# The first token group: four x transfers, applies on VectorE alone, w1's sums of squares added by TensorE

## The chip, the cores and the metric

The kernel runs on one core of a Trainium2 chip. A core has TensorE (PE: matmuls and transposes, results in PSUM), VectorE (DVE), ScalarE (ACT), GpSimd (POOL) and SyncE (SP, which here only issues transfers). Each engine works through its own instructions in order and waits for others by semaphores. The metric is the device time of one execution in microseconds, the median of several runs.

## The reference

The input x has 2048 tokens of 448 channels. Three things are added up:

```python
xn = layernorm(x)
y  = irfft2(rfft2(xn) * (w_r + 1j * w_i))        # spectral part
h  = gelu(layernorm(x) @ w1)                     # 448 x 448
hs = concat(shift(h[:, 0:112], +1), shift(h[:, 112:224], -1),
            shift(h[:, 224:336], +2), shift(h[:, 336:448], -2)) @ w2
x1 = x + hs
b  = x1 + gelu(layernorm(x1) @ w3) @ w4          # 448 x 1792 and back
out = x + y + b
```

The shifts are along the tokens. Everything is float32 outside; inside, each operand of a matmul is split into a high and a low float16 half, and three products (high x high, high x low, low x high) stand for one.

## The kernel before

Tokens are held as 16 blocks of 128 (token = 16 a + b, with a on the partitions and b the block), in four groups of four blocks, `GRP`. Group 0 is blocks 14, 15, 0, 1. Weights are scaled by a power of two before they are split: the scale comes from the sum of squares of the whole matrix (`squares` on ACT gives one sum per partition, `powers` adds them up over columns and partitions and makes the scale and its inverse from the exponent).

The part that is touched is the preamble, until the first matmul with w1, and goes like this:

- SP issues the loads in order (lines 195 to 223): x of group 0 in two transfers of two blocks each (line 200), w1 in four slices of up to 128 rows (lines 206 and 207), x of group 1, a second copy of w1's last slice, w2, x of group 2, w3, x of group 3. There are eight completion counters that are used in turn; a transfer waits until the one eight before it has landed.
- PE runs `WARM` = 22 matmuls on a zeroed tile, whose results nobody reads (line 890).
- `norm1(0, ...)`: DVE takes mean and variance of each block (lines 316 and 317), then four-element-wide operations: variance + eps in two forms (lines 342 and 343), a first guess of the inverse root by integer arithmetic in two instructions (344 and 345), minus mean times the guess (347). Then the blocks are normalised in place, x * y + m (the "applies"): block 14 on POOL, 15 and 0 on DVE (line 360), block 1 shared between POOL (128 columns, line 355) and ACT (320 columns, line 357). The refinement of the guess (`refine`) is done on POOL much later, and is folded into a scale after the matmul.
- Meanwhile ACT squares w1's four slices (`squares1`, line 246), each an activation with a read-out of its accumulator. Then `powers` (lines 248 to 266): a reduction over the columns on DVE (251), a matmul with a matrix of ones (258), which adds over partitions, and three operations on DVE: the exponent (261), the scale s1 (263), the inverse r1 (264).
- `warm_on` (line 943): one small matmul that reads the result of line 347, and two more warm-up matmuls behind it.
- `turn_pe(0, t)` transposes 128 columns of all four blocks on PE; `turn_copy` takes the high half out of PSUM on ACT (line 424) and the low half on DVE (425). `split_w` scales and splits w1's slices (lines 273 and 275 on DVE for the first slice, ACT and POOL for the others). The matmuls with w1 are at line 465.

Instructions are placed on the engines by the framework's planner, by program order and a timeline that it estimates; `with behind(...)` adds an order between two instructions of one engine without a wait between engines. In the preamble most of the order is fixed that way: the ones matmul stands behind the four transposes of `turn_pe(0, 0)` on PE, `turn_pe(0, 1)` behind the ones matmul, and the first w1 matmuls follow.

Of the kernel before, what the change touches and what calls it, by code (L numbers as in the profile page):

```python
# [12 lines left out]
F32 = mybir.dt.float32  # L13
F16 = mybir.dt.float16
I32 = mybir.dt.int32
AF = mybir.ActivationFunctionType
# [10 lines left out]
WARM = 22  # L27
# [95 lines left out]
def body(tc, nc, x, wf, w1, w2, w3, w4, c_g, c_n, c_small, out):  # L123
# [41 lines left out]
    def xb(b):  # L165
        g, i = WHERE[b]
        return xt[g][:, i]
# [27 lines left out]
    def load_x(g):  # L195
        if g:
            SY.dma_start(xt[g], xv[:, GRP[g][0]:GRP[g][0] + 4])
        else:
            for i in (0, 2):
                SY.dma_start(xt[g][:, i:i + 2], xv[:, GRP[g][i]:GRP[g][i] + 2])  # L200
# [47 lines left out]
    def powers(m, n, key, tag="acc", mid=None, pin=None, down=0):  # L248

        t = pc.tile([128, 1], F32, name=f"pt{key}")  # L250
        i = V.tensor_reduce(out=t, in_=m[:, :n + 1], axis=AX.X, op=ALU.add)
        after["t" + key] = (i.ins,)
        if mid:
            with behind("t" + key):
                mid()
        pm = bank(tag, f"pm{key}") if isinstance(tag, str) else tag
        with behind(*pin) if pin else contextlib.nullcontext():
            i = T.matmul(pm[:, 0:1], ones, t, start=True, stop=True)
        after["p" + key] = (i.ins,)
        e = pc.tile([128, 3], I32, name=f"pe{key}")  # L260
        V.tensor_scalar(out=e[:, 0:1], in0=pm.bitcast(I32)[:, 0:1], scalar1=1, scalar2=0x7F800000,
                        op0=ALU.logical_shift_right, op1=ALU.bitwise_and)
        V.tensor_scalar(out=e[:, 1:2], in0=e[:, 0:1], scalar1=-1, scalar2=(185 - down) << 23, op0=ALU.mult, op1=ALU.add)
        i = V.tensor_scalar(out=e[:, 2:3], in0=e[:, 0:1], scalar1=1, scalar2=(69 + down) << 23, op0=ALU.mult, op1=ALU.add)
        after["s" + key] = (i.ins,)
        return e.bitcast(F32)[:, 1:2], e.bitcast(F32)[:, 2:3]
# [28 lines left out]

    def rsqrt(r, a, n, key):
# [3 lines left out]
        V.tensor_single_scalar(i, a.bitcast(I32), 1, op=ALU.logical_shift_right)  # L300
        V.tensor_scalar(out=i, in0=i, scalar1=-1, scalar2=0x5F3759DF, op0=ALU.mult, op1=ALU.add)
# [29 lines left out]
    def norm1(g, apply, seen=0, mid=None):  # L331
# [8 lines left out]
        y = yi.bitcast(F32)  # L340
        with behind(0, 3) if g == 2 else contextlib.nullcontext():
            V.tensor_scalar(out=a[:, n:], in0=mv[:, :n, 1], scalar1=1.0 + EPS, scalar2=EPS * EPS, op0=ALU.mult, op1=ALU.add)
            V.tensor_scalar(out=a[:, 0:n], in0=mv[:, :n, 1], scalar1=EPS, scalar2=None, op0=ALU.add)
        V.tensor_single_scalar(yi, a.bitcast(I32), 1, op=ALU.logical_shift_right)
        V.tensor_scalar(out=yi, in0=yi, scalar1=-1, scalar2=0x5F3759DF, op0=ALU.mult, op1=ALU.add)
        nm = pc.tile([128, n], F32, name=f"nma{b0}")
        i = V.scalar_tensor_tensor(out=nm, in0=mv[:, :n, 0], scalar=-1.0, in1=y[:, n:], op0=ALU.mult, op1=ALU.mult)
        if mid:
            mid()
        for k, b in enumerate(bs):  # L350
            y_, m_ = y[:, n + k:n + k + 1], nm[:, k:k + 1]
            if apply[k] is A:
                o = 128 if g == 0 else 0
                if o:
                    P.tensor_scalar(out=xb(b)[:, :o], in0=xb(b)[:, :o], scalar1=y_, scalar2=m_, op0=ALU.mult, op1=ALU.add)
                with behind("sq", g) if ("sq", g) in after else contextlib.nullcontext():
                    i = A.activation(out=xb(b)[:, o:], in_=xb(b)[:, o:], func=AF.Identity, scale=y_, bias=m_)
                after["na", g] = (i.ins,)
            else:
                i = apply[k].tensor_scalar(out=xb(b), in0=xb(b), scalar1=y_, scalar2=m_, op0=ALU.mult, op1=ALU.add)  # L360
                after["n" if apply[k] is V else "np", g] = (i.ins,)

# [31 lines left out]
        return refine, gain, scales, nm  # L394
# [498 lines left out]
    m1, m2, m3, m4 = (pc.tile([128, n + 1], F32, name=f"m{i}") for i, n in ((1, 4), (2, 1), (3, 4), (4, 7)))  # L893
    junk4 = row().bitcast(F16)[:, :2 * D]
    for m, n in ((m1, 4), (m2, 1), (m3, 4), (m4, 7)):
        V.memset(m, 0.0)
        V.memset(m[:, n:], 2.0 ** -65)
# [61 lines left out]
    for t in range(4):  # L959
# [239 lines left out]
```

## Time and profile before

| what | value |
|---|---|
| median of 3 runs | 408.34 us (408.29 to 408.58) |
| profiled execution | 408.91 us, span 406.4 us |
| instructions | 8829 |
| PE busy | 401.0 us, 3379 matmuls |
| DVE, ACT, POOL busy | 304.0, 268.4, 173.0 us |
| granted TensorE clock | 1.00 |

The profile is of one execution; its span is from the first to the last instruction, and the time beside it includes what lies around. "PE" rows are matmuls, "PEld" rows are the loads of their stationary operands, "SPq" rows are issues of transfers. In a row of the timeline stand start, duration, engine, line, operation, output and input by the program's names, shape and count; in brackets is the idle time of the engine before it and what ended it. Where several instructions are put in one row, the duration is from the first's start to the last's end. A matmul's duration includes its way through the array, so that neighbours overlap: the distance of two starts is what one costs.

### The profile page before, as it was taken

What the parts mean: (1) busy time and instruction counts of PE and PEld (TensorE: products, weight loads), DVE (VectorE), ACT (ScalarE), POOL (GpSimd) and SP (SyncE); (2) the same over time, 40 slices, a digit from 0 to 9 for tenths busy, and PEclk for the clock granted to TensorE, in tenths of its full rate; (3) what the DMA queues carried; (4) which work ended last, traced back from release to release, by engine and by line L of the source; (5) the groups of instructions that cost most, each with busy time, mean ns of one, the idle gap of its engine ahead of it and who ended that gap; (6) DMA issues with size and microseconds to landing.
All of it is one profiled execution on the core that took longest, in us unless ns stands there. A gap on an engine that the chain in (4) does not pass through costs nothing.

```text
span 406.4 us, 8829 instructions
## 1 busy us (share of the span) xinstructions
PE 401.0 (99%) x3379; PEld 295.9 (73%) x3379; DVE 304.0 (75%) x664; ACT 268.4 (66%) x465; POOL 173.0 (43%) x270
## 2 busy tenths in 40 slices
PE   8999999999999999999999999999999999999996
PEld 3554556666677877776878878877788888888885
DVE  5989998898554757893677777773588879889645
ACT  4699984984738766862587888776856566444332
POOL 3889803011099746599143434431232264211000
PEclk9999999999999999999999999999999999999999
DMA  8999999905910383417064566632000112233201
GB/s 283 379 245 183 175 176 253 272 2 113 242 57 0 96 276 129 115 34 177 15 147 129 144 151 163 157 93 58 2 2 2 47 45 77 86 96 112 89 2 45
DMA packets 57209, 49.46 MB, mean 122 GB/s; under 512 B 41312, under 2 KB 52192, under 8 KB 57168
## 3 DMA queue, kind: packets, MB, share of 16 engines
q1 hardware_dynamic: 57168, 48.91, 46.1%
q8 instruction: 26, 0.43, 0.5%
q14 instruction: 15, 0.12, 0.1%
HBM read 35.06 MB, written 3.67 MB: 95 GB/s over the span
## 4 chain that ended last, share of the span: by engine, by line
PE 83%; DVE 7%; DMA 3%; ACT 3%; issue 1%; POOL 0%; SPq 0%; DVEq 0%; ACTq 0%
PE pw L435 28%; PE acc L812 22%; PE pw L510 8%; PE pw L465 6%; PE pu L708 3%; PE ps L605 3%; PE pp L662 2%; PE px L679 2%; PE cr L827 2%; PE acc L827 2%; DVE xr L560 1%; DMA out<-xr 1%; PE pe L728 1%; PE py L750 1%; DVE hf L778 1%
## 5 line engine op out<-in xcount | busy, mean ns | idle before, releaser
L435 PE MATMUL pw<-x2mem,w3p 128*128 128x256 f16 x1232 | 149.2, 272 | 0.0
L435 PEld LDWEIGHTS <-w3p 128*128 128x128 f16 x1232 | 118.8, 98 | 19.4
L812 PE MATMUL acc<-w4p,hf 128*128 128x448 f16 x508 | 107.6, 352 | 0.0
L812 PEld LDWEIGHTS <-hf 128*128 128x128 f16 x532 | 51.4, 98 | 35.4
L778 DVE SCALAR_TENSOR_TENSOR hf<-pw,h,hf 128x512 f16<-128x512 f32 x56 | 41.8, 747 | 37.0 <-ACT hf L777 36.8
L774 ACT ACTIVATE pw<-pw,pe 128x512 f32<-128x512 f32 x56 | 36.7, 656 | 42.7 <-PE pw L435 42.6
L777 ACT ACTIVATE hf<-pw,h 128x512 f16<-128x512 f32 x56 | 38.3, 684 | 1.3
L510 PE MATMUL pw<-w2p,h 112*128 112x448 f16 x192 | 39.0, 352 | 0.1
L735 POOL TENSOR_TENSOR e<-e 128x226 f32<-128x226 f32 x16 | 11.0, 688 | 64.0 <-ACT e L732 56.5
L465 PE MATMUL pw<-w1p,w4x 128*128 128x448 f16 x176 | 34.8, 352 | 0.5 <-DVE h L968 0.5
L510 PEld LDWEIGHTS <-h 112*128 112x128 f16 x192 | 18.6, 98 | 16.3 <-DMA h<-x2mem 0.9
L689 POOL TENSOR_TENSOR xr<-te 128x450 f32<-128x450 f32 x16 | 15.7, 981 | 34.1 <-DVE te L687 34.1
L465 PEld LDWEIGHTS <-w4x 128*128 128x128 f16 x176 | 17.0, 98 | 16.4 <-ACT w4x L424 0.7
L697 POOL TENSOR_TENSOR zb<-xr,zb 128x450 f16<-128x450 f32 x16 | 16.2, 1011 | 17.1 <-ACT zb L696 17.1
L742 ACT ACTIVATE vh<-e 128x448 f16<-128x448 f32 x16 | 9.2, 575 | 15.6 <-DVE e L740 15.4
L685 DVE SCALAR_TENSOR_TENSOR te<-px,sc,wc 128x450 f32<-128x450 f32 x16 | 11.0, 686 | 10.3 <-ACT te L684 6.7
L684 ACT ACTIVATE te<-px 64x450 f32<-64x450 f32 x32 | 17.3, 539 | 1.7 <-PE px L679 1.2
L720 ACT ACTIVATE U<-y 113x512 f16<-113x512 f16 x32 | 18.0, 620 | 0.1
L732 ACT ACTIVATE e<-pe 128x452 f32<-128x452 f32 x16 | 8.7, 544 | 12.7 <-PE pe L728 10.2
L712 DVE SCALAR_TENSOR_TENSOR y<-pu,y 113x512 f16<-113x512 f32 x16 | 10.9, 687 | 6.9 <-ACT y L711 6.8
L540 POOL TENSOR_SCALAR y<-xt,nm 128x448 f32<-128x448 f32 x6 | 5.9, 991 | 22.8 <-DMA x2mem<-y 12.9
L584 POOL TENSOR_TENSOR xr<-xf 128x452 f32<-128x452 f32 x6 | 6.7, 1123 | 20.6 <-ACT xf L580 10.5
(207 smaller groups left out, 793.1 us busy)
## 6 DMA issues: line engine op xcount, KB each, us to landing
wc<-wf SPq DMA_DIRECT2D x32, 225.0 KB, 3.8
wl<-wf SPq DMA_DIRECT2D x8, 450.0 KB, 3.9
xt<-x SPq DMA_DIRECT2D x3, 896.0 KB, 10.2
w3raw<-w SPq DMA_DIRECT2D x3, 896.0 KB, 14.0
xf<-x SPq DMA_DIRECT2D x6, 448.0 KB, 3.9
xr<-x SPq DMA_DIRECT2D x12, 224.0 KB, 2.5
out<-xr SPq DMA_DIRECT2D x12, 224.0 KB, 2.0
gn<-c_g SPq DMA_DIRECT2D x16, 128.0 KB, 3.1
```

The costliest lines, as they stand in the source:

```text
L435: m = T.matmul(ps_out, wp[:, wi + t, cols], xT[:, xi + t, tok], start=t == 0 and wi + xi == 0, stop=t == 3 and wi == 4)
L465: m = T.matmul(pm[:, :D], xTs[g][:, xi + t, 128 * i:128 * i + 128], w1p[:, wi + t], start=t == 0 and p == 0, stop=t == 3 and p == 2)
L510: m = T.matmul(w2b[b][:, :D], hT[g][:112, 4 * hi + k, o:o + 128], w2p[:, wi, k], start=k == 2 and hi + wi == 0, stop=k == 3 and hi == 1)
L684: i = A.activation(out=e[64 * h:64 * h + 64], in_=px_[64 - 64 * h:128 - 64 * h, :2 * DF], func=AF.Copy)
L689: P.tensor_tensor(out=z, in0=t[:, 0], in1=t[:, 1], op=ALU.add)
L697: P.tensor_tensor(out=zv[1], in0=z, in1=zv[0], op=ALU.subtract)
L720: A.activation(out=U[b][:113, p].rearrange("p q (c k) -> p q c k", c=NC), in_=Y1[:113, p, :, :, b], func=AF.Copy)
L774: A.activation(out=pm, in_=pm, func=AF.Gelu_apprx_tanh, scale=r3)
L777: i = A.activation(out=h[:, 0], in_=pv_, func=AF.Copy, scale=h3)
L778: j = V.scalar_tensor_tensor(out=h[:, 1], in0=pv_, scalar=h3, in1=h[:, 0], op0=ALU.mult, op1=ALU.subtract)
L812: m = T.matmul(to, h[:, hi, 2 * f + i], w4p[0][:, wi, 2 * fp + f, r], start=fp == s and f == 0 and hi + wi == 0, stop=fp == e and f == 1 a ...
L827: m = T.matmul(to, h[:, hi, slot] if slot < 4 else g[:, hi, slot - 4], w4f[fp][k][wi], start=k in (0, 6) and fp == 0 and hi == 0, stop=hi ...
```

## The change

- x of group 0 is loaded in four transfers of one block each.
- `WARM` goes from 22 to 15, and `warm_on` now reads the guess y.
- In group 0 all four applies are on DVE and compute (x - mean) * y, so that line 347's product isn't needed. Of the two forms of variance + eps only the one that the applies need is made before them, on four columns; the other and its guess follow behind the applies (`rough`, `guess`).
- In all groups, and in `rsqrt`, the guess is one instruction (times -0.5, plus a constant, on the integer) in place of two.
- w1's squares come in three activations: slice 0, slices 1 and 2 together (896 columns), slice 3. The reduction on DVE is gone for w1: PE adds the columns up, one ones matmul per column, accumulating in one PSUM column: the constant column and slice 0 ahead of the first transposes, the other two behind them.
- `powers` is cut in two; for w1 the inverse r1 is made behind the first scaled slice (line 273).

```diff
-WARM = 22
+WARM = 15
...
-            for i in (0, 2):
-                SY.dma_start(xt[g][:, i:i + 2], xv[:, GRP[g][i]:GRP[g][i] + 2])
+            for i, b in enumerate(GRP[g]):
+                SY.dma_start(xt[g][:, i], xv[:, b])
...
+    def factors(pm, key, down=0):
         e = pc.tile([128, 3], I32, name=f"pe{key}")
...
-        i = V.tensor_scalar(out=e[:, 2:3], in0=e[:, 0:1], scalar1=1, scalar2=(69 + down) << 23, op0=ALU.mult, op1=ALU.add)
...
+        def inverse():
+            i = V.tensor_scalar(out=e[:, 2:3], in0=e[:, 0:1], scalar1=1, scalar2=(69 + down) << 23, op0=ALU.mult, op1=ALU.add)
+            after["s" + key] = (i.ins,)
+            return e.bitcast(F32)[:, 2:3]
...
+    def guess(i, a):
+        V.tensor_scalar(out=i, in0=a.bitcast(I32), scalar1=-0.5, scalar2=0x5F3759DF, op0=ALU.mult, op1=ALU.add)
...
+            rough(1)
+            if g:
+                rough(0)
+        guess(yi[:, 0 if g else n:], a[:, 0 if g else n:])
+        if g:
+            V.scalar_tensor_tensor(out=nm, in0=mv[:, :n, 0], scalar=-1.0, in1=y[:, n:], op0=ALU.mult, op1=ALU.mult)
...
+                    i = apply[k].tensor_scalar(out=x_, in0=x_, scalar1=mv[:, k, 0:1], scalar2=y_, op0=ALU.subtract, op1=ALU.mult)
...
+        if not g:
+            with behind("n", 0):
+                rough(0)
+                guess(yi[:, 0:n], a[:, 0:n])
...
-    def squares1():
-        for t in range(4):
-            n = 128 if t < 3 else 64
-            i = squares(m1[:n, t:t + 1], w1s[:n, t])
-        after["sq", 0] = (i.ins,)
+    squares(m1[:, 0:1], w1s[:, 0])
+    squares(m1[:, 1:2], flat(w1s[:, 1:3]))
+    squares(m1[:64, 2:3], w1s[:64, 3])
...
-    n1 = [norm1(0, [P, V, V, A], mid=squares1)]
+    n1 = [norm1(0, [V, V, V, V])]
     warm_on(n1[0][3], 2)
-    pts = [turn_pe(0, 0)]
-    with behind("n", 0), behind("T", 0):
-        s1, r1 = powers(m1, 4, "1", "mm")
+    pm = bank("mm", "pm1")
+
+    def norm_of(ks):
+        for k in ks:
+            i = T.matmul(pm[:, 0:1], ones, m1[:, k:k + 1], start=k == 3, stop=k == 2)
+        after["p1"] = (i.ins,)
+
+    norm_of([3, 0])
+    with behind("p1"):
+        pts = [turn_pe(0, 0)]
+    with behind("T", 0):
+        norm_of([1, 2])
+    with behind("n", 0):
+        s1, r1 = factors(pm, "1")
     with behind("p1"):
         pts.append(turn_pe(0, 1))
...
+    with behind("w1", -1):
+        r1 = r1()
```

More of the change, by code (lines that the diff above doesn't have):

```diff
@@ L299, in rsqrt @@
         w = pc.tile([128, 8], F32, tag="nw", bufs=2, name=f"nw{key}")[:, :n]
-        V.tensor_single_scalar(i, a.bitcast(I32), 1, op=ALU.logical_shift_right)
-        V.tensor_scalar(out=i, in0=i, scalar1=-1, scalar2=0x5F3759DF, op0=ALU.mult, op1=ALU.add)
+        guess(i, a)
         y = i.bitcast(F32)
@@ L340, in norm1, with rough @@
         y = yi.bitcast(F32)
+        nm = pc.tile([128, n], F32, name=f"nma{b0}")
+        def rough(k):
+            V.tensor_scalar(out=a[:, n * k:n * k + n], in0=mv[:, :n, 1], scalar1=1.0 + EPS * k, scalar2=EPS ** (1 + k),
+                            op0=ALU.mult, op1=ALU.add)
         with behind(0, 3) if g == 2 else contextlib.nullcontext():
-            V.tensor_scalar(out=a[:, n:], in0=mv[:, :n, 1], scalar1=1.0 + EPS, scalar2=EPS * EPS, op0=ALU.mult, op1=ALU.add)
-            V.tensor_scalar(out=a[:, 0:n], in0=mv[:, :n, 1], scalar1=EPS, scalar2=None, op0=ALU.add)
@@ L350, in norm1 @@
+        if g:
+            V.scalar_tensor_tensor(out=nm, in0=mv[:, :n, 0], scalar=-1.0, in1=y[:, n:], op0=ALU.mult, op1=ALU.mult)
         for k, b in enumerate(bs):
-            y_, m_ = y[:, n + k:n + k + 1], nm[:, k:k + 1]
+            x_, y_, m_ = xb(b), y[:, n + k:n + k + 1], nm[:, k:k + 1]
             if apply[k] is A:
[L353 to L357, printed above, removed]
+                i = A.activation(out=x_, in_=x_, func=AF.Identity, scale=y_, bias=m_)
@@ L358, in norm1 @@
                 after["na", g] = (i.ins,)
             else:
-                i = apply[k].tensor_scalar(out=xb(b), in0=xb(b), scalar1=y_, scalar2=m_, op0=ALU.mult, op1=ALU.add)
+                if g:
+                    i = apply[k].tensor_scalar(out=x_, in0=x_, scalar1=y_, scalar2=m_, op0=ALU.mult, op1=ALU.add)
+                else:
+                    i = apply[k].tensor_scalar(out=x_, in0=x_, scalar1=mv[:, k, 0:1], scalar2=y_, op0=ALU.subtract, op1=ALU.mult)
                 after["n" if apply[k] is V else "np", g] = (i.ins,)
+        if not g:
+            with behind("n", 0):
+                rough(0)
+                guess(yi[:, 0:n], a[:, 0:n])
```

19 lines of the change are left out of this document (7 added, 12 removed).

## Prediction

> **What bounds the kernel now.** I read three views first: who TensorE (PE) waits for over the whole run, the chain that ended last, and PE's instructions in order of time.
>
> ```profile
> PE wps L890 <- DVE x2mem L188: 1.2, 1, 1.2
> PE pw L465 <- DVE h L968: 0.5, 1, 0.5
> PE cr L827 <- DVE hf L778: 0.3, 1, 0.3
> ```
> ```profile
> 12.91 6.81 PE pw L465 x36
> ```
> ```profile
> 11.12 0.92 PE L465 MATMUL pw<-w1p,w4x 128*128 128x448 f16 x4 [0.52 <-DVE h L968]
> ```
>
> In the first view the columns are total wait, number of waits, longest wait. It lists 2.0 us of waits in 406.4 us, and after 11.12 us only 0.3 us of them, near the end. The chain's row says that the w1 matmuls run at 6.81 / 36 = 0.189 us each without a hole. So the kernel is a preamble of 11.12 us and then a full PE. Whatever the first w1 matmul at 11.12 gains or loses is the change of the time, nearly one for one; a microsecond gained elsewhere in the preamble is worth nothing. The question is what ends last in front of that matmul.
>
> VectorE (DVE) in order of time, then ScalarE (ACT), each row with start, duration, engine, line:
>
> ```profile
> 4.48 1.15 DVE L316 BATCH_NORM_STATS2 sta<-xt 128x6 f32<-128x448 f32 x2 [2.97 <-DMA xt<-x]
> ...
> 7.14 0.17 DVE L342 TENSOR_SCALAR va<-mva 128x4 f32<-128x4 f32 x1
> 7.22 0.16 DVE L343 TENSOR_SCALAR va<-mva 128x4 f32<-128x4 f32 x1
> 7.41 0.17 DVE L344 TENSOR_SCALAR vy<-va 128x8 int32<-128x8 int32 x1
> 7.62 0.17 DVE L345 TENSOR_SCALAR vy<-vy 128x8 int32<-128x8 int32 x1
> 7.82 0.16 DVE L347 SCALAR_TENSOR_TENSOR nma<-mva,vy 128x4 f32<-128x4 f32 x1
> 8.02 1.26 DVE L360 TENSOR_SCALAR xt<-xt,vy,nma 128x448 f32<-128x448 f32 x2
> 9.21 0.14 DVE L251 TENSOR_REDUCE pt<-m 128x1 f32<-128x5 f32 x1
> 10.14 0.16 DVE L261 TENSOR_SCALAR pe<-pm 128x1 int32<-128x1 int32 x1 [0.79 <-PE pm L258]
> 10.33 0.15 DVE L263 TENSOR_SCALAR pe<-pe 128x1 int32<-128x1 int32 x1
> 10.40 0.14 DVE L264 TENSOR_SCALAR pe<-pe 128x1 int32<-128x1 int32 x1
> 10.52 0.45 DVE L273 TENSOR_SCALAR w1p<-w1s,pe 128x448 f16<-128x448 f32 x1
> ```
> ```profile
> 7.72 0.58 ACT L246 ACTIVATE xr<-w1s 128x448 f16<-128x448 f32 x1
> 8.20 0.19 ACT L246 ACTIVATION_READ_ACCUMULATOR xr<-w1s 128x1 f32 x1
> 8.42 0.58 ACT L246 ACTIVATE xr<-w1s 64x448 f16<-64x448 f32 x1
> 8.90 0.19 ACT L246 ACTIVATION_READ_ACCUMULATOR xr<-w1s 64x1 f32 x1
> 9.00 0.64 ACT L357 ACTIVATE xt<-xt,nma,vy 128x320 f32<-128x320 f32 x1
> ...
> 14.42 1.69 ACT L246 ACTIVATE xr<-w2s 112x1792 f16<-112x1792 f32 x1
> ```
> ```profile
> 5.03 0.15 PEld L890 LDWEIGHTS <-x2mem 128*128 128x128 f16 x1 [0.28 <-issue]
> 5.46 0.15 PEld L890 LDWEIGHTS <-x2mem 128*128 128x128 f16 x1 [0.28 <-issue]
> 5.84 2.04 PEld L890 LDWEIGHTS <-x2mem 128*128 128x128 f16 x10 [0.23 <-issue]
> ...
> 9.66 0.24 PEld L258 LDWEIGHTS pm<-pt,ones 128*128 128x128 f32 x1
> ```
>
> Two paths run side by side. The x path: first x lands (4.48), four statistics, five small operations (7.14 to 8.02), the applies, the last of them on ACT until 9.00 + 0.64 = 9.64, transposes. The w1 path: four squares on ACT until 8.90 + 0.19 = 9.09, their sum on DVE (9.21), the ones matmul that adds over partitions (weights at 9.66), three small operations, the scaled w1 slice (10.52 to 10.97), the first w1 matmul. They meet at 9.66: the sum was ready at 9.21 + 0.14 = 9.35, but PE takes its instructions in order and the ones matmul stands behind the fourth transpose, which waits for the apply that ends at 9.64. So today the x path sets the time, with the w1 path 0.3 us behind it. From 9.66 the rest is fixed: 0.48 to the first exponent operation (10.14), 0.98 from there to the matmul.
>
> **The change part by part.** When does w1 reach ACT? The DMA queue's rows (SP), its waits, and bytes by half microsecond (last columns: DMA share, GB/s):
>
> ```profile
> 0.73 0.87 SPq L200 DMA_DIRECT2D xt<-x  x2
> ...
> 7.65 0.33 SPq L197 DMA_DIRECT2D xt<-x  x1
> ```
> ```profile
> SPq L197 <- DMA w1s<-w: 0.5, 1, 0.5
> ```
> ```profile
> 2.00:2.50 0.50, 0.50 (x3) 0.18 (x2) 0.00 (x0) 0.21 (x2) 0.50 (x2) 1.00 0.34 50
> 2.50:3.00 0.50, 0.50 (x3) 0.22 (x2) 0.00 (x0) 0.00 (x0) 0.09 (x1) 1.00 0.71 194
> ...
> 4.00:4.50 0.50, 0.50 (x2) 0.15 (x1) 0.02 (x1) 0.00 (x0) 0.00 (x0) 1.00 1.06 430
> ...
> 6.00:6.50 0.50, 0.50 (x5) 0.20 (x3) 0.50 (x2) 0.23 (x1) 0.00 (x0) 1.00 1.05 402
> ```
>
> The x transfer of a later group sits at 7.65 because its completion counter is the one w1's third slice uses: that slice landed just before 7.65, and ACT starts its square at 7.72. So the third and fourth squares already run as soon as their data or ACT allow.
>
> *Four transfers for x.* The same 0.92 MB, in rows of 1792 bytes where two blocks side by side gave 3584. Two more issues at 0.87 / 2 = 0.44 us move every later issue of SP's queue by 0.87 us. That is hidden: the queue is far ahead of the data (w1's issue, then near 1.7, is used at 6.27 and later), and the counters, used in turn, stay paired for w1 and the later loads because both extra transfers stand in front. If that cover were gone it would cost up to 0.87. For the first block, half the bytes: at 430 GB/s, 229 KB is 0.53 us less; in the slow start (50, then 194 GB/s from 2.0 to 3.0) it can be nothing. I take 0.43 earlier, bounds 0 and 0.6. For w1, behind x, there is a loss: w1's own 1792-byte rows run at 402 GB/s where x's 3584-byte rows run at 430, so x takes 0.92 MB x (1/402 - 1/430) = 0.15 us longer. If the slow start counts packets and not bytes, the 122 KB moved from 2.0 to 3.0 become 61 KB, another 0.15. Call the delay of w1's landing k: bounds 0 and 0.35 with its completion work, taken 0.25, nearer the upper end because w1's rows are the very size x now gets.
>
> For a price of small transfers the Trainium skill, "DMA: Bandwidth & Descriptors" (section "Anatomy of one DMA"), fits about 2.0 us plus bytes / 436 GB/s, and its "Specifications" put line rate at 512 bytes and up. By that page the row length costs nothing, k is 0, and the sum below would come to 408.2; the 402 against 430 GB/s in this trace is the opposite sign, so I go by the rows.
>
> *Shorter chain.* L343 leaves the chain (it starts 0.08 after L342), L344 and L345 become one, L347 goes: from L342 to the apply there were 0.88 us, now two dependent steps of 0.20 (7.41 to 7.62): 0.40. Gain 0.48 on the x path. The two operations that moved behind the applies come back as 0.4 us of DVE, under the wait for the ones matmul (0.79 idle today).
>
> *All applies on DVE.* Two take 8.02 to 9.21, so 0.60 each beside a POOL apply; L273, as wide with fp16 out and POOL idle, takes 0.45. Four cost 1.8 to 2.4. Start: 8.02 - 0.43 - 0.48 = 7.11; last end 8.9 to 9.5. That is 0.1 to 0.7 before today's 9.64, and ACT and POOL lose their shares of it.
>
> *w1's squares.* Two slices are squared in one instruction, 896 wide. By 0.58 for 448 and 1.69 for 1792, 896 takes 0.58 + 1.11 x 448/1344 = 0.95, that is 0.37 more than one, and saves one square with its read-out (8.42 - 7.72 = 0.70). But the pair can't start before the later of its slices: 7.72 + k, exactly where the third square starts now. So it is not a saving. Last square: 8.42 + 0.37 + k = 8.79 + k, read out after 0.67: 9.46 + k, against 9.09. Late by 0.37 + k.
>
> *Sums by PE.* L251 goes, with its hand-overs: the ones matmul for the last column starts about 0.05 after ACT (as 9.66 stands 0.02 behind 9.64), at 9.51 + k. The columns that come sooner add matmuls of the same kind, while PE waits anyway. With k = 0.25 it starts at 9.76; bounds 9.51 and 9.86.
>
> *The late inverse.* L264 starts at 10.40, inside the 0.19 that L273 (10.52) waits for L263 anyway (10.33, as 10.33 waits for 10.14). Gain 0. Behind L273 it costs DVE 0.07 before the low half of x, needed only after four matmuls and eight transposes; hidden.
>
> *Fewer warm-up matmuls.* Seven at 2.04 / 10 = 0.20 us each; the ten of the row at 5.84 end by 7.9 and are in nobody's way. They must end earlier now that the transposes may start near 7.7. The shorter guess in the later groups saves DVE about 0.2 us each, off PE's path (0.3 us of waits in all): 0, at most 0.2.
>
> **Sum.** The ones matmul goes from 9.66 to 9.76: +0.10 us (bounds -0.15 and +0.20). The x path is done by then either way. So the path that sets the time changes hands: x is ready earlier, and w1's sums, later by the fused square and k, use it up. The profiled execution took 408.91 us (span 406.4), 0.57 above the median of 408.34. Its own time would be 409.0; the median's, 408.45.
>
> **The rivals.**
>
> *The w1 path is not late.* If small packets are free and the pair of slices lands with less of a tail, the x path keeps setting the time: its last apply at 8.9, the ones matmul at 8.92, that is 0.74 earlier: 407.6. With the bounds of the x path (0.6 for 0.43) it is 0.91: 407.4, the first value beyond 0.2%. It needs w1's third slice by about 7.1 in place of 7.65. The transfer row speaks against it, since bytes in front of w1 don't become fewer.
>
> *The clock falls back (slower).* PE's warm-up weights are 0.43 us apart until 5.46 and 0.20 from 5.84 on: the array runs at half its pace for the first 4.6 us of work. With 15 warm-ups PE is done with them near 6.7 and then has only small matmuls and eight transposes, with holes of about half a microsecond, until 11.2. If that is too little activity, the w1 matmuls start at 0.38 in place of 0.19. It decides once the pace falls at all; price half the time until it recovers: up to 2.3 us for another 4.6. Against it: today's hole of 0.52 before 11.12 left the pace at 0.189. I price it at 1.7: 410.1. The Trainium skill, "TensorE: Matmul & The Clock Gate" (section "Part 1: The HAM clock gate"), has the same halving, after an idle window of about 3.4 us; no hole that I foresee is as long, and by that rule the price is 0, or half of 3.4.
>
> *A new stall further on (slower).* The instructions are ordered by a planner, and other times in the preamble may shift neighbours on DVE or POOL that a later matmul needs. PE has no slack: a delay of 0.8 us or more there ends at 409.3 to 410. For it speaks only that PE is full; against it, that the order around the first group is pinned by hand.
>
> **How the numbers follow.** Forecast as summed: 0.60. w1 path not late: 0.20, of which 0.12 beyond 0.2%. Clock: 0.08. New stall: 0.10. The remaining 0.02 is small and of no sign. About 0.2%, 0.8 us here, is what a measurement of this kernel can tell from no change: faster than 407.5 has 0.12, slower than 409.2 has 0.18, between them 0.70. The likeliest case alone spans 408.2 to 408.7. The range 407.4 to 409.6 takes in the x path's bound below and the smaller stalls above; some 0.05 below and 0.12 above are left out.
>
> **What would show it.** In the profile after: first statistics near 4.05 and first apply near 7.1; four DVE applies at 0.45 to 0.6; the wide square starting near 7.9 and taking 0.95; the last read-out ending near 9.7, and the last ones matmul right behind it, with the transposes of x waiting for nothing. The first w1 matmul near 11.2. I am wrong if the wide square starts near 7.0, if the ones matmul starts before 9.3, if w1 matmuls stand 0.38 apart, or if PE shows waits after 11.2 that sum to over 0.5 us.

## The result, and the profile after

The changed kernel takes 412.50 us (median of 6, 411.67 to 413.57) against 408.49 for the kernel before beside it: a ratio of 1.0095, 95% interval 1.0076 to 1.0113. It is slower by about 4.0 us, where the forecast was 408.45 with 409.6 as the upper end. The profiled execution is the longest of the six: 413.57 us, its span 411.8 (before: 408.91 and 406.4). The mean granted clock of the six is 0.991 to 0.999; the one at 0.999 took 411.80, so the clock that is read below is not the whole loss. Lines of the changed kernel have other numbers: L246 are the squares, L326 and L327 the statistics, L354 and L305 the rough variance and the guess, L373 the applies, L970 the ones matmuls, L431 the transposes, L482 the w1 matmuls.

SP's own queue shows the landings, because from the ninth transfer on each waits for the one eight places before it (start, duration, line):

```profile
6.43 0.34 SPq L210 DMA_DIRECT2D w2s<-w  x1
7.71 0.35 SPq L197 DMA_DIRECT2D xt<-x  x1
8.74 0.94 SPq L217 DMA_DIRECT2D w3raw<-w  x2
10.01 0.33 SPq L197 DMA_DIRECT2D xt<-x  x1
```

The third and fourth x block have landed at 6.4 and 7.7, w1's first slice at 8.7, its third at 10.0; before, that third slice was there at 7.65. The stretches (from:to, then length, busy time and count for PE, PEld, DVE, ACT, POOL, then granted clock, DMA share and GB/s) show how. First before, then after:

```profile
3.00:4.50 1.50, 1.50 (x5) 0.51 (x4) 0.02 (x1) 0.00 (x0) 0.00 (x0) 1.00 0.99 382
4.50:6.00 1.50, 1.50 (x5) 0.55 (x4) 1.50 (x5) 0.00 (x0) 0.00 (x0) 1.00 1.01 391
```
```profile
3.00:4.50 1.50, 1.50 (x5) 0.51 (x4) 1.09 (x3) 0.00 (x0) 0.00 (x0) 1.00 0.91 240
4.50:6.00 1.50, 1.50 (x5) 0.55 (x4) 0.15 (x2) 0.00 (x0) 0.00 (x0) 1.00 0.92 259
...
7.00:9.20 2.20, 0.00 (x0) 0.00 (x0) 1.52 (x8) 0.39 (x1) 0.00 (x0) 1.00 1.07 331
9.20:11.20 2.00, 1.67 (x6) 1.21 (x7) 1.83 (x6) 1.36 (x5) 0.00 (x0) 0.50 1.03 331
...
14.00:16.00 2.00, 2.00 (x7) 1.18 (x8) 2.00 (x6) 1.07 (x2) 1.72 (x4) 0.50 1.11 186
```

The engines are 0.91 busy and still move only 240 GB/s where they moved 382. PE has nothing to do from 7.0 to 9.2, and from 9.2 on its clock is 0.50. DVE, ACT and PE in order of time:

```profile
3.41 1.15 DVE L326 BATCH_NORM_STATS2 sta<-xt 128x6 f32<-128x448 f32 x2 [1.90 <-DMA xt<-x]
...
6.43 0.63 DVE L326 BATCH_NORM_STATS2 sta<-xt 128x6 f32<-128x448 f32 x1 [1.79 <-DMA xt<-x]
...
7.71 0.63 DVE L326 BATCH_NORM_STATS2 sta<-xt 128x6 f32<-128x448 f32 x1 [0.57 <-DMA xt<-x]
...
8.59 0.17 DVE L354 TENSOR_SCALAR va<-mva 128x4 f32<-128x4 f32 x1
8.80 0.17 DVE L305 TENSOR_SCALAR vy<-va 128x4 int32<-128x4 int32 x1
9.00 1.78 DVE L373 TENSOR_SCALAR xt<-xt,mva,vy 128x448 f32<-128x448 f32 x4
```
```profile
10.09 0.95 ACT L246 ACTIVATE xr<-w1s 128x896 f16<-128x896 f32 x1 [0.61 <-DMA w1s<-w]
10.95 0.19 ACT L246 ACTIVATION_READ_ACCUMULATOR xr<-w1s 128x1 f32 x1
11.17 0.58 ACT L246 ACTIVATE xr<-w1s 64x448 f16<-64x448 f32 x1
11.65 0.19 ACT L246 ACTIVATION_READ_ACCUMULATOR xr<-w1s 64x1 f32 x1
```
```profile
9.53 0.59 PE L970 MATMUL pm<-m,ones 128*128 128x1 f32 x2 [2.55 <-ACT xr L246]
...
12.07 0.85 PE L970 MATMUL pm<-m,ones 128*128 128x1 f32 x4
12.78 1.09 PE L431 MATMUL pta<-ident,xt 128*128 128x128 f32 x4
13.94 1.65 PE L482 MATMUL pw<-w1p,w4x 128*128 128x448 f16 x4
...
16.58 3.76 PE L482 MATMUL pw<-w1p,w4x 128*128 128x448 f16 x19
```

Before, the second stretch of w1 matmuls stood here:

```profile
12.75 6.97 PE L465 MATMUL pw<-w1p,w4x 128*128 128x448 f16 x36
```

The first x block comes sooner (3.41 for 4.48), the third and fourth do not; the wide square waits for w1's slice until 10.09. The first w1 matmul stands at 13.94 for 11.12: +2.82 us. The first four matmuls with the eight transposes behind them take 2.64 us (13.94 to 16.58), before 1.63 (11.12 to 12.75): +1.01, because at half clock the matmuls stand 0.37 apart for 0.19 and the transposes are slower too. The rest are PE's later waits:

```profile
PE pm L970 <- ACT xr L246: 2.5, 1, 2.5
...
PE ps L622 <- DVE xh L613: 0.6, 1, 0.6
PE pw L527 <- DMA h<-hs: 0.5, 2, 0.3
```

Both lower rows are new. By the distances of PE's starts, holes of more than 0.1 us behind these matmuls sum to 2.3 us against 0.8 before: +1.5. Together 2.82 + 1.01 + 1.5 = 5.3, of 5.4 us between the spans of these two executions; the medians lie 4.0 apart.

### The profile page after: what moved, and what is told of

Read it like the earlier page. It is cut to its first block, busy times and chain, and to the rows that moved or that the text cites. A ratio compares the mean times of both kernels' runs of the same rounds, so it can differ in the third digit from the quotient of the medians.

```text
span 411.8 us, 8812 instructions
## 1 busy us (share of the span) xinstructions
PE 403.5 (98%) x3378; PEld 298.0 (72%) x3378; DVE 303.5 (74%) x656; ACT 267.6 (65%) x462; POOL 169.8 (41%) x268
## 4 chain that ended last, share of the span: by engine, by line
PE 81%; DMA 6%; DVE 5%; ACT 3%; POOL 2%; issue 2%; SPq 0%; POOLq 0%; ACTq 0%
PE pw L452 29%; PE acc L829 19%; PE pw L482 6%; PE pw L527 4%; PE cr L844 4%; PE acc L844 3%; PE pu L725 3%; PE ps L622 2%; PE pp L679 2%; PE pe L745 2%; PE px L696 2%; PE py L767 2%; DMA h<-hs 2%; DMA xt<-x 1%; DMA x2mem<-w 1%
## 5 line engine op out<-in xcount | busy, mean ns | idle before, releaser
L482 PE MATMUL pw<-w1p,w4x 128*128 128x448 f16 x176 | 35.5, 357 | 0.1
L482 PEld LDWEIGHTS <-w4x 128*128 128x128 f16 x176 | 17.1, 99 | 16.5 <-issue 0.9
L749 ACT ACTIVATE e<-pe 128x452 f32<-128x452 f32 x16 | 8.7, 545 | 13.3 <-PE pe L745 11.0
L613 DVE TENSOR_TENSOR xh<-xf,xh 128x452 f16<-128x452 f32 x12 | 11.7, 1004 | 6.0 <-ACT xh L612 6.0
```

Of the source, the lines that this page charges most:

```text
L482: m = T.matmul(pm[:, :D], xTs[g][:, xi + t, 128 * i:128 * i + 128], w1p[:, wi + t], start=t == 0 and p == 0, stop=t == 3 and p == 2)
```

## The experiments

Each group below ran on one chip with the kernel before beside it; "before" times differ from chip to chip by up to 0.7 us, so each time is compared within its group.

### Which part carries the loss: e1 to e4 (before: 408.79)

**e1**, the change with x in two transfers again; **e2**, the kernel before with x in four, and nothing else:

```diff
-            for i, b in enumerate(GRP[g]):
-                SY.dma_start(xt[g][:, i], xv[:, b])
+            for i in (0, 2):
+                SY.dma_start(xt[g][:, i:i + 2], xv[:, GRP[g][i]:GRP[g][i] + 2])
```

> The changed kernel with x in two transfers again, everything else as changed. Theory A (the four x transfers are what costs: the third and fourth block and all of w1 land 2 us late, and PE's wait and half clock follow from that): w1's third slice lands near 7.65 again, first w1 matmul near 11.0, time 407.7 to 408.6. Theory B (the fewer warm-up matmuls let the clock fall, and that costs): still w1 matmuls 0.37 apart near 11, time 409.5 to 411. Theory C (the order of later work changed and new stalls there cost): 409.5 to 411 with w1 matmuls 0.19 apart.

> The kernel before with only the x transfers changed from two to four. Theory A: third and fourth x block land near 6.4 and 7.7, w1's third slice near 10, first w1 matmul about 2.5 to 3 us later than 11.1, time 411 to 412 (the 22 warm-up matmuls end by 8.4, so the clock may hold). Theories B and C: w1 lands within 0.3 us of before, time 408.3 to 408.8.

e1: 409.24, ratio 1.0016 (1.0006 to 1.0027), first w1 matmul at 11.31, 0.19 apart, full clock. e2: 410.84, ratio 1.0050 (1.0031 to 1.0069), first w1 matmul at 12.37. So the four transfers alone lose 2.05 us with nothing else changed, and the change without them loses 0.45. (Two of e2's five executions have a mean clock of 0.995 and 0.992; the three at full clock took 410.13 to 411.00.) In the stretches of e2's profile a poor rate stands too, at full clock:

```profile
3.00:4.50 1.50, 1.50 (x5) 0.50 (x4) 1.10 (x3) 0.00 (x0) 0.00 (x0) 1.00 0.98 262
4.50:6.00 1.50, 1.50 (x6) 0.61 (x5) 0.15 (x3) 0.00 (x0) 0.00 (x0) 1.00 0.91 306
```

**e3**, the change with `WARM = 22`; **e4**, the change with four transfers of another cut: 64 partitions by two blocks, rows of 3584 bytes.

> The changed kernel with 22 warm-up matmuls again. Theory A: w1 still lands near 10, first w1 matmul still near 13.9; at most the 1.0 us of half clock in the first four w1 matmuls and the transposes is won back: 411.3 to 412.3. Theory B: w1 matmuls 0.19 apart and 408.3 to 409.5.

> The changed kernel with four x transfers that each take 64 partitions of two blocks: as many transfers as changed, but rows of 3584 bytes as before. If the number of transfers costs: late landings as changed, 411.5 to 413.5. If the rows of single blocks cost (1792 bytes out of every 28672): first two transfers land near 4.4, the others near 5.6, w1's third slice near 7.7, time 407.7 to 408.8.

e3: 412.04, ratio 1.0074 (1.0051 to 1.0096). Its profile has the data as late as the change: w1's third slice landed at 9.98 (9.99), the last read-out ended at 11.83 (11.84). But the clock was full until 13.24, and the first w1 matmul stands at 13.28 for 13.94:

```profile
11.64 0.19 ACT L246 ACTIVATION_READ_ACCUMULATOR xr<-w1s 64x1 f32 x1
```
```profile
13.28 1.65 PE L482 MATMUL pw<-w1p,w4x 128*128 128x448 f16 x4 [0.52 <-DVE w1p L281]
```

So 0.66 of the 2.82 us in front of w1 are the half clock as well (it slows the ones matmuls and the transposes there), and the clock's price in the change's profiled execution is 0.66 + 1.01 = 1.7 us. From 13.24 to 16.65 e3's clock halved too, though PE had had no hole of more than 0.52 us; two of its four executions show it (0.995 and 0.996). So 22 warm-ups don't hold the clock when the data is late. e4: 412.40, ratio 1.0086 (1.0067 to 1.0104), its transfers land 0.9 to 1.0 us apart at 265 and 228 GB/s, and all four executions have a mean clock of 0.990 to 0.992. Long rows don't help; but with 64 neighbouring partitions this cut changes two things, so it was taken up again in e8.

### Rows, squares, guesses: e5 to e8 (before: 408.93)

**e5** is e1 with the two-instruction guess back in `rsqrt`; **e6** is e5 with the four single squares back; **e7** is the kernel before, x in two transfers of blocks that are no neighbours, so in rows of 1792 bytes; **e8** is the kernel before, x in four transfers, even and odd partitions of each pair, in rows of 3584 bytes.

> The changed kernel with x in two transfers, and with the guess inside rsqrt (the second layernorm) in two instructions again. With x in two transfers alone the w1 start was 11.31 against 11.12 and a new PE wait of 0.9 us stood near 117 us. Theory D (the shorter guess in rsqrt makes the planner order the second layernorm's small operations otherwise, the loads behind it go out 2 us later, and PE waits for the folded x near 117): the wait near 117 is gone, time 0.6 to 1.0 us below that kernel, 0.1 to 0.5 below the kernel before. If the wait has another cause it stays and the time is as with x in two transfers alone.

> As the run above, and w1's squares in four instructions again, one per slice, still added up by PE. By the prediction's terms the wide square ends 0.37 us later than four narrow ones; with four the last read-out is near 9.1 and the x path (last apply near 9.3 to 9.5) sets the ones matmul: w1 start 0.2 to 0.4 us earlier than in the run above, time lower by as much. If the fused square isn't late, no difference.

> The kernel before with x in two transfers of the same size, but of blocks that aren't neighbours (14 with 0, 15 with 1), so in rows of 1792 bytes like the changed kernel's. If the rows of 1792 bytes at a distance of 28672 slow the transfers: w1's third slice lands after 9 us and the first w1 matmul is at 12 or later, 410 us or more. If it is the number of transfers: w1 lands within 0.4 us of before, first w1 matmul by 11.6, under 409.3.

> The kernel before with four x transfers in rows of 3584 bytes: each pair of blocks in two transfers, even and odd partitions. If the number of transfers costs: w1's third slice after 9 us, first w1 matmul at 12 or later. If the rows cost: within 0.4 us of before, 408.3 to 409.3.

| run | time | ratio | GB/s 3.0-4.5, 4.5-6.0 | w1's third slice landed | first w1 matmul |
|---|---|---|---|---|---|
| e5 | 409.77 | 1.0025 (1.0014-1.0037) | 397, 375 | 7.36 | 10.94 |
| e6 | 409.77 | 1.0019 (1.0008-1.0029) | 404, 379 | 7.96 | 11.16 |
| e7 | 409.64 | 1.0024 (1.0010-1.0039) | 392, 376 | 8.32 | 11.95 |
| e8 | 411.76 | 1.0070 (1.0043-1.0097) | 313, 278 | 8.98 | 12.08 |

e7's short rows run at 392 GB/s like before's long ones (382), and e8's long rows in four transfers at 313 and 278. So the count of transfers on the queue costs, not the row. (e7 still gets w1 0.7 later than before. About half of that is scatter: in the eight profiled executions with x in the two transfers of before, w1's third slice landed between 7.36 and 8.02. The rest is open. e8's issues on SP also take longer, and w1's first goes out at 3.27 for 1.66.) The trace has the slow packets themselves. Between 3.2 and 6.0 us, packets of x and w1 that took over 0.25 us, where a packet of 1792 bytes takes 0.074 in the median: before 3, e7 2, e8 22, e2 15, the change 23. Those 23 hold 13.3 us of the engines' time. e6 misses its gain; it needs one more ones matmul behind the transposes, and its third slice also landed 0.6 us later than e5's, so one profile each can't say what four single squares are worth. e5 still has the stall near 117, so the guess in `rsqrt` is not its cause.

### The later stall, the queue and the clock: e9 to e12 (before: 408.79)

**e9**, the kernel before with only this:

```diff
-        V.tensor_single_scalar(yi, a.bitcast(I32), 1, op=ALU.logical_shift_right)
-        V.tensor_scalar(out=yi, in0=yi, scalar1=-1, scalar2=0x5F3759DF, op0=ALU.mult, op1=ALU.add)
+        V.tensor_scalar(out=yi, in0=a.bitcast(I32), scalar1=-0.5, scalar2=0x5F3759DF, op0=ALU.mult, op1=ALU.add)
```

**e10**, e5 with the two instructions kept in `norm1` for groups 1 to 3, so only the first group's part of the change is left.

> The kernel before, with one edit: the two-instruction first guess of the inverse root in the norm of x (L344, L345) becomes one instruction, in all four groups. This is the only part of the change that shows in the planned order of DVE behind the first group. Theory A (the shorter guess in the later groups makes the planner choose another order, in which the last DMA transposes of the second norm come 2 us later): the PE stall of about 0.9 us near 117 appears, and the time is 0.6 to 1.1 us above before's. Theory B (the stall comes from the changes in the first group: POOL and ACT relieved, late inverse, other matmuls): no stall there, and 0 to 0.2 us below before, from the 0.2 us shorter chain of the first group.

> The changed kernel with x in two transfers and the two-instruction guess kept everywhere but in the first group: what is left of the change is the first group's own. The planned order of DVE behind it is before's. Theory A: the stall near 117 is gone, the first w1 matmul stands at 10.9 to 11.3 (two runs with x in two transfers had 10.94 and 11.31), and the time is that of before plus the shift of this matmul: -0.2 to +0.2 us. Theory B: the stall stays, and the time is 0.6 to 0.9 us above before's, as with x in two transfers alone.

PE and SP of e9, then of e10:

```profile
117.30 0.29 PE L604 MATMUL ps<-csm,xh 128*128 128x128 f16 x2
118.16 1.69 PE L604 MATMUL ps<-csm,xh 128*128 128x128 f16 x22 [0.58 <-DVE xh L595]
```
```profile
106.57 1.56 SPq L574 DMA_DIRECT2D xf<-x  x3
```
```profile
117.01 1.50 PE L627 MATMUL ps<-csm,xh 128*128 128x128 f16 x24
```
```profile
104.63 2.12 SPq L597 DMA_DIRECT2D xf<-x  x3
```

The stall is in e9 and gone in e10: with one instruction less per group the planner puts the small operations of the second norm in another order, the last DMA transposes go out later, the loads of the folded x stand behind them (106.57 for 104.63), and DVE has `xh` late. The place is shown; the price of e9 missed its expectation: 408.67, ratio 1.0006 (0.9998 to 1.0015), because 0.24 us was gained in front (first w1 matmul 10.88, though x also landed 0.18 sooner there) and a hole of 0.42 us near 377 in before's trace is not in e9's. Between e9 and e10 lies 1.03 us. e10 took 407.64, ratio 0.9977 (0.9960 to 0.9994): faster than before.

**e11**, the kernel before with x in four transfers, two of them issued by ACT; **e12**, the change with `WARM = 34`:

```diff
-                SY.dma_start(xt[g][:, i], xv[:, b])
+                (A if i % 2 else SY).dma_start(xt[g][:, i], xv[:, b])
```

> The kernel before with x in four transfers, of which the second and the fourth are issued by ACT and not by SP. With all four on SP's queue the last w1 slice landed at 9.73 (before: 8.26) and the time was 2.05 us above before's. Theory Q (one queue takes on the next transfer only some 0.6 us after the last, so the number of transfers ahead of w1 on its queue counts): with two of them elsewhere w1's last slice lands at 8.2 to 8.7, the first w1 matmul stands before 11.6, and the time is at most 0.5 us above before's. Theory E (each further transfer costs the engines the same wherever it is issued): last slice near 9.7, first w1 matmul near 12.3, 1.5 to 2.1 us above before's.

> The changed kernel with 34 warm-up matmuls in place of 15, so that PE works until about 10.8. Theory C (PE's hole from 6.99 to 9.53 halved the clock, and this cost 1.0 us): the clock stays full, the first w1 matmuls stand 0.19 apart, the first of them at 13.5 to 14.0, and the time is 0.9 to 1.4 us below the changed kernel's 412.5, that is about 411.3. Theory N (the wait for the late data is what costs, and PE's pace is only its companion): the clock holds, but the time stays within 0.3 us of 412.5.

e11: 408.13, ratio 0.9994 (0.9979 to 1.0008), last w1 slice at 8.59 (e2: 9.73), 4 slow packets (e2: 15), first w1 matmul at 11.10. The loss of e2 is gone, with the same blocks in the same rows:

```profile
3.00:4.50 1.50, 1.50 (x5) 0.51 (x4) 0.04 (x1) 0.00 (x0) 0.00 (x0) 1.00 1.04 385
4.50:6.00 1.50, 1.50 (x6) 0.60 (x5) 1.50 (x4) 0.00 (x0) 0.00 (x0) 1.00 1.05 376
```

The Trainium skill, "Trainium Kernel Development and Optimization" (section "Key Constraints"), says that issuing from several engines only saves the sequencer's issue time. What is saved there is 2.60 - 1.65 = 0.95 us of w1's first issue, while the rate differs by nearly a half from 3.0 to 4.5 (385 for 262 GB/s) and by a quarter from 4.5 to 6.0. Here the measurement decides, with one doubt that e13 takes up: e11 also sends w1's issues out as early as before.

e12: 411.27, ratio 1.0069 (1.0055 to 1.0084), as expected. The clock holds, the matmuls stand 0.19 apart:

```profile
13.33 0.92 PE L482 MATMUL pw<-w1p,w4x 128*128 128x448 f16 x4 [0.52 <-DVE w1p L281]
```
```profile
14.00:16.00 2.00, 2.00 (x16) 1.48 (x15) 2.00 (x4) 1.28 (x3) 2.00 (x4) 1.00 0.94 222
```

From the first w1 matmul to the second stretch (14.96) it is 1.63 us as before, in the change 2.64; by the ratios, 0.0026 of 408.8, e12 is 1.1 us better than the change. The intervals overlap, e12's data also landed 0.76 us sooner, and its 34 warm-ups themselves hold PE until 11.0, so the profile carries the figure: 1.0 us for the pace from the first w1 matmul on, with the 0.66 in front of it that e3 shows.

### Issue or transfer, and whether the parts add up: e13 to e15 (before: 408.87)

**e13**, the kernel before with two issues of one row each between x and w1:

```diff
     load_x(0)
+    for i in range(2):
+        SY.dma_start(x2mem.bitcast(F32)[0:1, D * i:D * i + D], w1[i:i + 1])
```

> The kernel before, with two more issues on SP between x and w1, each of one row of 1792 bytes into a place that is written much later: x stays in two transfers, and w1's issues come about 0.8 us later. Theory I (what made w1 late with four x transfers is the time of its issue on SP): w1's last slice lands 0.8 to 1.5 us after before's 8.26 and the time is 0.8 us or more above before's. Theory T (it is the transfers themselves, full-size ones that start one after the other on one queue, and the issues are hidden): w1's last slice lands by 8.7, and the time is at most 0.4 us above before's.

Neither theory is met. w1's third slice landed at 8.24 (before 7.64, e2 9.18), the first w1 matmul stands at 11.45 (before 11.12, e2 12.37). The rate from 3.0 to 6.0 stays at 394 and 350 GB/s. w1's issues in e13, then in e2 (before: from 1.66 on):

```profile
2.29 1.30 SPq L208 DMA_DIRECT2D w1s<-w  x3
```
```profile
2.60 1.38 SPq L206 DMA_DIRECT2D w1s<-w  x3
```

In e13 the landing is late by about as much as the issue (0.60 and 0.63), and 8.24 lies only 0.2 beyond the scatter named above. e2's issue is late by 0.94, so issues alone could make up to 0.9 of its 1.54 us; the split is not shown. They don't explain x itself: e2's third and fourth block went out at 1.66 and 2.12 and landed 4.3 and 4.75 us later, where the first took 2.65. But the time is 411.20, ratio 1.0053 (1.0036 to 1.0071): 2.3 us lost. In the profiled execution (412.25) most of it is behind the preamble, where PE waits at 31 us for a transpose of hs and then runs 3.41 us at half clock:

```profile
PE pw L512 <- DMA h<-hs: 2.0, 1, 2.0
```

Two transfers more in front also shift whom the later ones wait for: x of group 1 is issued at 4.55 for 3.65, w2 at 6.17 for 4.79, x of group 2 at 6.79 for 5.59, and all land later. In their profiles e2 and the change have such holes too, two of about 0.4 us each between 32 and 36; e3 and e12, also with four transfers, do not.

**e14**, e10 with w1's second and third slice in one transfer; **e15**, the whole change with the two queues of e11.

> The first-group-only kernel (x in two transfers, the later guess in two instructions; 407.64), with w1's second and third slice in one transfer, which the fused square needs together anyway: one transfer fewer ahead of the fourth slice. Its chain waits for the landing of the third slice (7.69). If each start of a transfer on the queue costs the landing, the pair lands at 7.3 to 7.6 and the first w1 matmul comes 0.1 to 0.4 us sooner than its 10.99: 407.3 to 407.6. If only bytes count, the pair lands at 7.7 and the time is the same within 0.15 us.

> The whole change, but with the second and fourth x transfer issued by ACT. If the four transfers cost only through the one queue, everything that hung on them goes: PE is idle for less than 1.5 us before the ones matmul, the clock stays full, the first w1 matmul stands at 11.0 to 11.5, and what is left over the kernel before is the stall near 117 from the later shorter guess: 408.8 to 409.6. If the other parts of the change lose on their own, or the clock falls with 15 warm-ups anyway, it stays above 410.5.

e14: 409.07, ratio 1.0012 (0.9997 to 1.0027): the pair landed at 8.28, its engines spread over 1.4 us. One transfer fewer was no gain, so a price per start alone is not the mechanism. (Five of the 12 executions, at 409.67 to 410.95, have a mean clock of 0.995 or 0.996; the others took 408.21 to 409.40.) e15: 410.29, ratio 1.0041 (1.0020 to 1.0061), by the ratios 2.2 us better than the change, first w1 matmul at 11.12 and full clock in the profiled execution, but above the 408.8 to 409.6 expected: besides the stall near 119 it has holes of 0.48, 0.60 and 0.30 us between 19 and 33, again where later loads are used.

### Settling the first group's part: e16, e17 (before: 408.93) and e18 (before: 409.16)

**e16** is e10 again, **e17** is e10 with x in four transfers on two queues, **e18** is e10 with `WARM = 22`.

> The first-group-only kernel once more (x in two transfers, later guess in two instructions), beside the next one on one chip. If its gain is its own: first w1 matmul at 10.8 to 11.1, no stall near 117, 0.4 to 1.2 us below before. If its 407.64 was the luck of that chip's transfers: within 0.3 us of before.

> The same kernel with x in four transfers, the second and fourth issued by ACT: the whole change but for the shorter guess in the later groups. If the parts add up, it lies 0.8 to 1.4 us below the whole change on two queues (410.29), that is at 408.9 to 409.5: no stall near 117, the first w1 matmul at 11.0 to 11.3, and what it loses against the two-transfer kernel are PE waits between 19 and 37 us, because the loads behind the first eight are issued about 0.5 to 1 us later (each waits for the landing of the transfer eight places before it). If four transfers on two queues cost nothing, it lies within 0.3 us of the two-transfer kernel.

> The first-group-only kernel (407.64 and 408.15) with before's 22 warm-up matmuls in place of 15. With 15, four of its 24 executions had a granted clock of 0.995 or 0.996, and these took 409.0 to 409.5, against 407.4 to 408.5 for the others. If the shorter warm-up leaves PE's clock on an edge, no execution of this kernel is below 0.997, all lie below 408.9, and the median is 0.5 to 1.2 us under before's. If the clock falls for another reason, one or two of twelve have it still. The ones matmul stands behind 1.4 us more of warm-ups, which end near 9.0, before its data is there: the first w1 matmul stays at 10.9 to 11.3.

e16: 408.15, ratio 0.9981 (0.9970 to 0.9991): the gain holds on another chip, though its profiled execution has the first w1 matmul at 11.32. e17: 408.59, ratio 1.0002 (0.9978 to 1.0025), 407.65 to 411.97, so wide that it can't be told from e16. 1.7 us lie between it and e15, of which the later order explains about 1.0; the parts add up only roughly. Its profile shows something else, the granted clock in the third column from the end:

```profile
7.00:9.20 2.20, 1.95 (x10) 1.02 (x11) 2.10 (x7) 1.30 (x3) 0.00 (x0) 1.00 0.97 341
9.20:11.20 2.00, 1.33 (x10) 1.00 (x11) 1.15 (x5) 1.51 (x5) 0.59 (x1) 1.00 1.05 290
11.20:14.00 2.80, 2.80 (x12) 1.95 (x11) 2.80 (x7) 1.14 (x3) 2.80 (x5) 0.52 1.01 305
```

The clock fell at 11.31 for 3.41 us with PE busy for most of the time before. Four of the 24 executions of e10 and e16, with 15 warm-ups, have a mean clock of 0.995 or 0.996, as one such spell gives, and took 409.0 to 409.5; the others took 407.4 to 408.5. In e18 none of 12 has it: 408.39, ratio 0.9984 (0.9973 to 0.9996), one of them above the 408.9 expected, with 409.27 at full clock. That alone does not show that the shorter warm-up is the reason: with a rate of 4 in 24, none in 12 comes by chance one time in nine. The other groups say more. With 15 warm-ups and x in two transfers, e1 and e6 had none in 22, e5 had 3 in 12 and e14 5 in 12, so with e10 and e16 it is 12 in 70. With 22 warm-ups and x in the same two transfers, e9, e18 and the kernel before in all groups together had 1 in 159. That points strongly to the shorter warm-up, but only e18 changes nothing else.

What is shown is that the first group's part of the change, with x in two transfers and the later guess as it was, is faster than the kernel before in three groups of runs (e10, e16, e18), by 0.16 to 0.23%.

## Why the prediction was wrong

- *What bounds.* Right as a frame: PE is full behind the first w1 matmul, and its shift is the largest term. "Nearly one for one" was too bold: 1.01 us of clock and 1.5 us of later waits came on top of 2.82. One reading was wrong, without harm: the fourth transpose at 9.66 waited for POOL's 128 columns of block 1, until 9.60, and not for ACT's 320, until 9.64:

```profile
9.03 0.57 POOL L355 TENSOR_SCALAR xt<-xt,vy,nma 128x128 f32<-128x128 f32 x1
```

- *Four transfers for x.* This is the step that failed, by its size. I took k, the delay of w1's landing, as 0.25 with 0.35 as the upper end, from 402 against 430 GB/s for short rows. It measured 1.54 alone (e2: third slice 9.18 for 7.64) and 2.35 in the change (9.99); e12 and e3, with the same transfers, have 1.59 and 2.34. My 0.25 was smaller than the scatter of this landing with x in two transfers (7.36 to 8.02). The reason I gave is not the cause: short rows run at full rate (e7), and there the Trainium skill's line rate from 512 bytes up, in "DMA: Bandwidth & Descriptors" (section "Specifications"), agrees with 392 GB/s in e7. The k of 0 that I worked out from that page does not hold in the change, and the fit that I took from it (section "Anatomy of one DMA") is given there for DMAs that GpSimd issues, where these are issued by SP. What I left out is how four transfers share one queue. "That is hidden" of the two issues failed twice: with next to no data they come with a landing 0.6 later (e13), and they move the later loads, whose counters I called paired though x of group 1 and w2 now wait for others.
- *First block earlier.* 0.43 taken, 1.07 measured (3.41 for 4.48), outside my bound of 0.6. It was worth nothing, since the chain needs all four blocks, and the fourth came at 7.71.
- *Shorter chain, applies on DVE.* Right: two steps of about 0.2 (8.59, 8.80, 9.00), four applies in 1.78, under the 1.8 to 2.4 I gave. In e9, with the shorter guess alone, DVE's step is gone as forecast; of the 0.24 us in front, x's sooner landing has a share.
- *The fused square and PE's sums.* Right: 0.95 for the wide square, and "9.46 + k" for the last read-out gives 11.81 with k = 2.35; it ended at 11.65 + 0.19 = 11.84. With k = 0.05, in e10, the sum says -0.10 for the ones matmul and the first w1 matmul moved by -0.13 (10.99). The sum puts the first w1 matmul at 11.12 + 0.10 - 0.25 + k = 10.97 + k. e1, e10, e14, e16 and e18 stand within 0.05 us of it, and so does e3 with the late data (13.28 for 13.31). (e5, whose w1 landed before x was ready, and e12, whose warm-ups held PE, stand later.) The change stands 0.62 behind it (13.94 for 13.32), by its half clock. So the sum was sound; its one unknown was not.
- *Fewer warm-ups: nothing.* Probably wrong. With the data late, 22 didn't hold the clock either (e3) and 34 did (e12); with x in two transfers, 15 held it in 58 of 70 executions and 22 in 158 of 159, of which only e18's 12 differ from e10 in nothing but the warm-ups.
- *The clock rival* (0.08) came true, in its mechanism and, in the profiled execution, at its price: 0.66 + 1.01 us for the 1.7 I gave. It came on top of the late data, not in its place. Its reason against was that a hole of 0.52 us had left the pace alone. In the change PE's hole was 2.55 us, because the data was late; but in e3 and e17 the clock fell behind holes no longer than 0.52. The Trainium skill, "TensorE: Matmul & The Clock Gate" (section "Part 1: The HAM clock gate"), names an idle window of about 3.4 us. The spells agree with such a window (3.41 us in e17, 6.82 in the change), but the holes before them were shorter than it.
- *The stall further on* (0.10) came true as well, at 117, through the part I had priced at "0, at most 0.2": the shorter guess in the later groups.
- *The rival that w1 is not late* did not come true, though e10, e16 and e18, without the four transfers, gain 0.8 to 1.15 us where it had 0.74 to 0.91; that the sizes meet is luck. In e10 the last read-out ends at 9.54, behind the applies (7.28 + 1.78 = 9.06), so w1's path sets the time, and the first w1 matmul stands at 10.99, 11.32 and 11.00 in the three, for 11.12. The gain in these profiles is mostly later holes of PE in before's trace (0.24 us at 33, 0.42 at 377) that e10's and e16's lack. e11's lacks them too, with the first group's chain of before, so they need not hang on this part of the change; why they go is open.

Why four transfers on one queue make single packets slow is not settled. Shown is that it needs the four on one queue (e2, e8 against e11) and not the short rows (e7). How much of w1's delay comes from its later issue and how much from the transfers is not separated: 0.6 of 1.5 us by e13, up to 0.9 by e2's own issue times.

## What to carry to other kernels

Cutting a load so that its first piece comes sooner is paid by everything behind it on the same queue: read the GB/s of the stretch and the landing of the last piece that the chain needs, not that of the first. Where transfers share a set of completion counters, a transfer more in front changes when each later load is issued, and that shows tens of microseconds on. In a kernel whose order a planner writes, an edit that is meant for one place is best kept from all others, and a cover of warm-up matmuls is best sized for the latest data, not for the median: a slice's landing here moved by up to 0.66 us between executions with the same transfers.

## What the runs showed of the hardware that was not expected

- Four transfers of 229 KB on one queue ran at 240 and 259 GB/s in the change and at 262 and 306 in e2, with the engines over 0.9 busy; the same four on two queues at 385 and 376 (e11). Landings of one transfer over the 16 engines then spread by 2.1 us (third x block of the change, 4.27 to 6.41), against 0.4 to 0.6 for x before. In e4, with 64 partitions a transfer, the spread was 0.5 to 0.8 at no better rate, so the spread alone is not what costs.
- TensorE's clock fell without a long hole: at 11.31 in e17 and at 13.24 in e3, for 3.41 us each, after 3.4 us in which PE was busy for 2.54 and 2.46 us with warm-ups, ones matmuls and transposes. In e2 it stayed full behind a stretch as long with 2.36. So the busy share alone does not tell. In the change it fell at 9.21, 2.2 us into the hole of 2.55, and stayed at half for 6.82. PE's busy time is the second number, the granted clock the third from the end (e17, e3, e2):

```profile
7.89:11.31 3.42, 2.54 (x15) 1.58 (x15) 2.53 (x9) 2.90 (x7) 0.70 (x1) 1.00 1.06 346
```
```profile
9.83:13.24 3.41, 2.46 (x15) 1.50 (x13) 2.03 (x9) 2.63 (x6) 0.41 (x1) 1.00 1.02 274
```
```profile
8.92:12.33 3.41, 2.36 (x14) 1.22 (x13) 2.06 (x9) 3.21 (x9) 1.75 (x3) 1.00 1.04 299
```
